# Two roots of the first batch's norms on GpSimd as a power, in an attention and MLP kernel on one core

## The chip, the core and the metric

The kernel runs on one core of a Trainium2 chip. The metric is the device time of one execution in microseconds (us). A profile is one execution recorded by the hardware profiler; its span is a little shorter than the device time of the same execution. The engines are called PE (TensorE, matrix products), ACT (ScalarE, activation functions), DVE (VectorE), POOL (GpSimd) and SP (SyncE, which here only issues DMAs). Each engine works through its own instructions in the order in which they were written and waits on semaphores for the others.

## The reference

For each of 8 batches and 12 heads, q and k (448 rows of 64) are divided by the root of their mean square and multiplied by a gain; then softmax attention over 448 keys; the heads are put side by side and pass through an MLP of 768 to 2048 to 768 with a tanh GELU.

```python
def rmsnorm(x, g):
    rms = np.sqrt(np.mean(x * x, axis=-1, keepdims=True) + 1e-06)
    return x / rms * g
q_n, k_n = (rmsnorm(q, g_q), rmsnorm(k, g_k))
scores = (1.0 / np.sqrt(64)) * np.matmul(q_n, k_n.transpose(0, 1, 3, 2))
attn = softmax(scores)                     # max subtracted, 1e-9 in the sum
x = np.matmul(attn, v)                     # to (8 * 448, 768)
h = x @ w_in
g = 0.5 * h * (1.0 + np.tanh(c * (h + 0.044715 * h * h * h)))
return g @ w_out
```

## The kernel before

The 12 heads of a batch are taken as 6 pairs, and the pairs as three chunks of two: pair `i` belongs to chunk `c = i // 2`, with `j = i % 2`. For every pair the kernel squares the raw q and k, sums the squares along the 64 elements of a row, takes the inverse root, multiplies the raw rows by it and writes bf16, transposes the result with PE, and copies it from PSUM into `qT` and `kT` (k takes the gain on the way). Then come the scores (PE, 7 tiles of 128x896 for two pairs), their exponentials (ACT), the sums over keys and the products with v (PE), reciprocals (DVE), and the product into `xT`. The MLP of a batch is interleaved with the attention of the next.

The first batch has nothing before it that could be interleaved. Its instructions are written in an order by hand, a string `FRONT` of steps that `front` (line 669) turns into instructions; each step is issued to its engine when it is read, so the string fixes the order on each engine. The steps that matter here, each followed by the number of its pair:

- `sq`, `sk`: squares of q and k (line 186 on ACT, line 188 on POOL); `tq`, `tk`: their sums on DVE (line 203).
- `rs`: the inverse root of one pair's norms, `rsqrt` (line 205): on ACT `Ln(ssq / 64 + 1e-6)` into `lg` (line 209), then `Exp(-0.5 * lg)` into `rinv` (line 212). For an even pair it covers 14 columns, for an odd one 16, of 128 partitions: 8 for q and 6 or 8 for k.
- `nk`, `nq`: the multiplication by `rinv`, written to `nrmk` and `nrmq` (line 226), on DVE (`:D`) or POOL (`:P`).
- `tpk`, `tpq`: PE transposes (lines 245 and 238); `ck`, `cq`: the copies out of PSUM on DVE (lines 264 and 255).
- `s`, `e`: scores of a tile on PE (lines 324 and 310) and their exponential on ACT (line 331); `sa`, `sb`, `xa`, `xb`: halves of the key sums and of the products with v on PE (line 370).
- `st`, `rc`, `rb`, `xt`: reciprocals and the product into `xT` on DVE (lines 377, 381, 385, 395).
- `v`, `w`, `o`, `V`: DMAs that POOL issues: v of batch 0, a quarter of `w_in` (line 630), a part of `w_out` (line 636), v of batch 1.
- `ma`, `mb`, `mc`, `md`: matrix products of the MLP of batch 0 (line 412).

The string around pairs 4 and 5, which are chunk 2:

```python
        sq4:P sq5:P w1 rc0 cq3:D rb0 ck3:D tq4 tk5 rs4 e9 xb0 s10 st1 xt0 rc1 rb1 tq5 e10 sa2
        s11 e11 rs5 nk4:P nq4:P w2 nk5:P nq5:P xa1 xb1 sb2 s12 e12 s13 tpk4 tpq4 xt1 st2 ck4:D
        cq4:D rc2 xa2 e13 rb2 sa3 xb2 s14 tpk5 tpq5 s15 e14 xt2 ck5:D cq5:D sb3 e15 U s16 s17
        xa3 xb3 s18 w3 o0 Sk0:P e16 st3 rc3 rb3 e17 xt3 e18 s19 sa4 xa4 sb4 xb4 Tk0 st4 rc4 s20
        mb0 mb1 mb2 mb3 sa5 e19 e20 o1 Sq0:P Sq1:P V0 rb4 GELU xt4 Tq0 xa5 sb5 xb5 st5 V1 V2 o2
```

`Sk`, `Sq`, `Tk`, `Tq`, `Rs` are the same squares, sums and roots for batch 1. POOL's instructions around the change are thus, in order: `sq4 sq5 w1 nk4 nq4 w2 nk5 nq5 w3 o0 Sk0 o1 Sq0 Sq1 V0 ...`, and PE's are `s12 s13 tpk4 tpq4 xa2 sa3 xb2 s14 tpk5 tpq5 s15 sb3 s16 s17 ...`. `rsqrt` is called for chunk 2 of batch 0 by `rs4` and `rs5` alone. Other batches take all their roots in one or two calls.

Of the kernel before, what the change touches and what calls it, by code (L numbers as in the profile page):

```python
# [8 lines left out]
F32 = mybir.dt.float32  # L9
BF16 = mybir.dt.bfloat16  # L10
AF = mybir.ActivationFunctionType
ALU = mybir.AluOpType
# [4 lines left out]
def kernel(  # L17
# [11 lines left out]
    nc = tc.nc  # L29
    B, H, S, D = q.shape  # L30
# [19 lines left out]
    consts = ctx.enter_context(tc.tile_pool(name="consts", bufs=1))  # L50
# [11 lines left out]
    op = ctx.enter_context(tc.tile_pool(name="op", bufs=3))  # L62
# [37 lines left out]
    kT = consts.tile([128, NCH, NS, 128], BF16)  # L100

    NU = 4 * CH + 2 * NS
    ssq = [consts.tile([128, NCH, NU], F32, name=f"ss{i}") for i in range(3)]
    raws, sqs, rinvs, nrms = {}, {}, {}, {}
    qT, xT = {}, {}
# [98 lines left out]

    def rsqrt(b, c=slice(0, NCH), at=slice(0, NU)):
        if b not in rinvs:
            rinvs[b] = smp.tile([128, NCH, NU], F32, tag="rinv", name="rinv")
        lg = smp.tile([128, NCH, NU], F32, tag="lg", name="lg")
        nc.scalar.activation(
            lg[:, c, at], ssq[b % 3][:, c, at], AF.Ln, scale=1.0 / D, bias=eps  # L210
        )
        nc.scalar.activation(rinvs[b][:, c, at], lg[:, c, at], AF.Exp, scale=-0.5)  # L212
# [397 lines left out]
    nc.vector.memset(ones, 1.0)  # L610
    nc.vector.memset(rows, 1.0)
    nc.vector.memset(ssq[0], 1.0)
    nc.gpsimd.memset(onesr, 0.0)
    for j in range(2):
        nc.gpsimd.memset(onesr[own(j), j], 1.0)
# [53 lines left out]
    def front(step):  # L669
# [7 lines left out]
        elif name in ("tq", "tk"):  # L677
            total(0, c, n, j)
        elif name == "rS":
            rsqrt(0, i, slice(0, 30))  # L680
        elif name == "rs":
            rsqrt(0, c, slice(14 * j, 14 + 16 * j))
        elif name in ("nq", "nk"):
            normed(0, c, n, j, eng)
# [46 lines left out]
        elif name == "o":  # L731
            w_out_part(i // 2, slice(i % 2 * nf // 2, (i % 2 + 1) * nf // 2))
        elif name == "L":
            loads(*divmod(i, 10))
        elif name in ("Sq", "Sk"):
            square(1, i, n, eng)
        elif name in ("Tq", "Tk"):
            total(1, i, n)
        elif name == "Rs":
            rsqrt(1, slice(0, 2))  # L740
        elif name in ("Nq", "Nk"):
            normed(1, i // 10, n, i % 10, eng)
        elif name == "Tp":
            tps["Q", i] = trans(1, i, "q", ps_o, "o")
            tps["K", i] = trans(1, i, "k", ps_m, "mm")
        elif name in ("Cq", "Ck"):
            (place_q if n == "q" else place_k)(1, i, tps[n.upper(), i], eng)
        elif name in ("GELU", "EXP"):
            nc.scalar.preload_act_table_set(EXP_SET if name == "EXP" else GELU_SET)
        elif name == "mb":  # L750
            mm1(0, [0, 1], [i], act=False)
        elif name in ("ma", "mc", "md"):
            fs = [2 * i, 2 * i + 1] if i < 7 else [i + 7]
            cs = {"ma": range(4), "mc": [4], "md": [5] if i < 3 else range(HP)}[name]
            mm1(0, fs, cs, act=False)
        elif name == "g":
            gelu(0, [2 * i, 2 * i + 1] if i < 7 else [i + 7])
        else:
            raise ValueError(step)
# [176 lines left out]
```

## Time and profile before

| what | value |
|---|---|
| time, median of 3 runs | 413.02 us (412.62 to 413.85) |
| the profiled execution's time | 413.83 us |
| its span | 412.1 us |
| mean granted clock of PE in it | 0.992 |
| busy: DVE | 274.3 us (67%) |
| busy: ACT | 296.2 us (72%) |
| busy: POOL | 131.8 us (32%) |

In the lines of the profile shown below, L226 is line 226 of the kernel. A row of a timeline gives the start in us, the duration in us, the engine, the line, the operation, what it writes and reads, how many instructions were merged into the row, and in brackets how long the engine had been idle before it and who released it. POOLq, SPq and ACTq are an engine's issuing of DMAs. A row of the chain of waits gives start, duration and what the chain ran through. The granted clock (PEclk) is the share of PE's full clock that its throttle let through. Matmuls are pipelined, so a row's duration can reach past the start of the next.

### The profile page before, as it was taken

To read this page: it belongs to the slowest core of one execution; us is meant where nothing else is said; L and a number is where in the kernel's file an instruction comes from. 1 tells how busy PE (TensorE), PEld (TensorE's weight loads), DVE (VectorE), ACT (ScalarE), POOL (GpSimd) and SP (SyncE) were. 2 spreads that over 40 slices of the span, in tenths; PEclk is the share of its full clock that TensorE was granted. 3 is DMA by queue.
4 is the path that set the end of the run, shared out by engine and by line. 5 is a ranking of instruction groups with operands and counts; after the bars stand their busy time and mean duration, and the time that the engine had idled before them with its cause. 6 is when DMAs were issued, how large, how long until landed. Compare 5 with 4: busy or idle time off the path is not lost.

```text
span 412.1 us, 10085 instructions
## 1 busy us (share of the span) xinstructions
PE 403.7 (98%) x4207; PEld 243.5 (59%) x4207; DVE 274.3 (67%) x454; ACT 296.2 (72%) x398; POOL 131.8 (32%) x144
## 2 busy tenths in 40 slices
PE   8799999999999999999999999999999999999996
PEld 3344555566655666557655666556655575556664
DVE  4899739899899638884678747786488633783010
ACT  5797987969988587767977778785976558774300
POOL 7689000234500942037500745019310460000000
PEclk9699999999999999999999999999999999999999
DMA  8999995999981689229981399616991161210022
GB/s 191 227 235 228 203 196 141 227 227 192 213 145 38 139 176 207 66 52 176 222 140 41 78 203 171 136 40 145 171 145 40 23 112 40 72 46 2 2 77 78
DMA packets 97870, 54.21 MB, mean 132 GB/s; under 512 B 63776, under 2 KB 94368, under 8 KB 97824
## 3 DMA queue, kind: packets, MB, share of 16 engines
q1 hardware_dynamic: 71392, 41.69, 43.4%
q0 software_dynamic: 26112, 11.80, 22.5%
q8 instruction: 33, 0.54, 0.6%
q10 hardware_dynamic: 320, 0.07, 0.1%
q14 instruction: 13, 0.11, 0.1%
HBM read 45.61 MB, written 11.01 MB: 137 GB/s over the span
## 4 chain that ended last, share of the span: by engine, by line
PE 95%; SPq 2%; DMA 1%; DVE 0%; ACT 0%; issue 0%; ACTq 0%; DVEq 0%
PE o L441 36%; PE hh L412 31%; PE o L370 11%; PE sc L324 8%; PE h L412 5%; PE sc L310 1%; DMA rawq<-in_q_dram 1%; PE ox L370 1%; SPq L143 1%; SPq L118 1%; SPq L136 1%; PE tp L245 0%; PE o L477 0%; PE tp L238 0%; ACT ex L331 0%
## 5 line engine op out<-in xcount | busy, mean ns | idle before, releaser
L441 PE MATMUL o<-wout,g 128*64 128x384 bf16 (+1 forms) x1648 | 160.6, 327 | 0.0
L331 ACT ACTIVATE ex<-sc,shift 128x896 bf16<-128x896 f32 x144 | 136.1, 1011 | 1.3 <-PE sc L324 1.3
L412 PE MATMUL hh<-xT,win 128*64 128x448 bf16 (+1 forms) x1260 | 133.8, 353 | 0.0
L441 PEld LDWEIGHTS <-g 128*64 128x64 bf16 (+1 forms) x1648 | 96.2, 109 | 58.3 <-issue 14.8
L412 PEld LDWEIGHTS <-win 128*64 128x64 bf16 (+1 forms) x1440 | 95.4, 109 | 49.9 <-issue 3.2
L421 ACT ACTIVATE g<-hh 128x896 bf16<-128x896 f32 x56 | 50.1, 919 | 44.5 <-PE hh L412 44.4
L203 DVE TENSOR_REDUCE ss<-sq 128x14 f32<-128x896 f32 (+4 forms) x45 | 47.9, 1080 | 32.4 <-ACT sq L186 19.9
L454 ACT COPY osb<-o 128x384 f32<-128x384 f32 x50 | 24.2, 483 | 47.8 <-PE o L441 47.8
L788 POOL COPY mark<-es 1x1 bf16<-1x1 bf16 x8 | 1.8, 225 | 162.9 <-DVE es L345 158.5
L377 DVE STREAM_TRANSPOSE st<-o 128x448 f32<-128x448 f32 x48 | 31.1, 648 | 23.6 <-PE o L370 23.2
L324 PE MATMUL sc<-qT,kT 64*128 64x448 bf16 (+1 forms) x372 | 39.6, 360 | 1.7 <-DVE kT L264 1.3
L345 DVE TENSOR_TENSOR es<-ex 128x896 bf16<-128x896 bf16 x42 | 26.8, 637 | 12.0 <-ACT ex L331 12.0
L226 POOL TENSOR_TENSOR nrmq<-rawq,rinv 112x512 bf16<-112x512 f32 x33 | 34.0, 1043 | 0.0
L226 POOL TENSOR_TENSOR nrmk<-rawk,rinv 128x512 bf16<-128x512 f32 (+1 forms) x33 | 31.1, 957 | 4.2 <-ACT rinv L212 4.2
L385 DVE STREAM_TRANSPOSE rb<-rc 128x448 f32<-128x448 f32 x48 | 31.0, 645 | 1.6
L370 PE MATMUL o<-ex,vb 128*64 128x448 bf16 x252 | 30.9, 352 | 0.0
L279 DVE TENSOR_SCALAR kT<-kT,gcol 128x896 bf16<-128x896 bf16 x19 | 21.1, 1108 | 11.7 <-DMA kT<-nrmk 11.7
L343 DVE TENSOR_TENSOR es<-es,exr 64x896 bf16<-64x896 bf16 x42 | 25.9, 617 | 2.4 <-ACT exr L331 1.0
L345 DVE TENSOR_TENSOR es<-es,ex 128x896 bf16<-128x896 bf16 x42 | 25.5, 608 | 2.3 <-ACT ex L331 0.3
L395 DVE TENSOR_TENSOR xT<-o,rb 128x448 bf16<-128x448 f32 x42 | 25.8, 615 | 1.4 <-PE o L370 0.9
L188 POOL TENSOR_TENSOR sq<-rawq 112x1024 f32<-112x1024 f32 x9 | 17.0, 1893 | 28.4 <-DMA rawq<-in_q_dram 25.0
L324 PEld LDWEIGHTS <-kT 64*128 64x128 bf16 (+1 forms) x372 | 10.9, 99 | 24.6 <-issue 18.1
(83 smaller groups left out, 349.4 us busy)
## 6 DMA issues: line engine op xcount, KB each, us to landing
rawq<-in_q_dram SPq DMA_DIRECT2D x48, 224.0 KB, 4.4
rawk<-in_k_dram SPq DMA_DIRECT2D x48, 192.0 KB, 4.6
vb<-in_v_dram POOLq DMA_DIRECT2D x8, 576.0 KB, 10.1
win<-in_moe_w_in_dram POOLq DMA_DIRECT2D x4, 768.0 KB, 14.1
wout<-in_moe_w_out_dram POOLq DMA_DIRECT2D x4, 768.0 KB, 20.4
out_dram<-osb SPq DMA_DIRECT2D x7, 336.0 KB, 4.3
out_dram<-osb SPq DMA_DIRECT2D x8, 288.0 KB, 2.7
out_dram<-osb SPq DMA_DIRECT2D x8, 240.0 KB, 2.6
```

Of the source, the lines that this page charges most:

```text
L203: nc.vector.reduce_sum(stat(ssq[b % 3], b, c, n, j), view(n, sqs[n, b, c], j), axis=AX.X)
L226: eng.tensor_mul(dst.rearrange("p t a d -> p a t d"), view(n, raws[n, b, c], j), r.to_broadcast(list(r.shape) + [D]),)
L324: nc.tensor.matmul(sc[o, a, :S], kT[r, c, 4 * j + t, o], qT[b][r, hp], start=True, stop=True,)
L331: nc.scalar.activation(dst, sc[:, :, :S], AF.Exp, scale=scale, bias=shift)
L343: nc.vector.tensor_add(es[p], es[p], exrs[b, hp // 2][p])
L345: nc.vector.tensor_add(es, ex[:, 0] if t == 1 else es, ex[:, t])
L370: nc.tensor.matmul(o[a * D:(a + 1) * D], w(a), e[:, a], start=(i == 0), stop=(i + 1 == len(steps)),)
L377: nc.vector.transpose(oas["st"].rearrange("p a b -> p (a b)"), oas[0])
L385: nc.vector.transpose(oas["rb", hp], oas["rc"].to_broadcast([128, S // 32, 32]))
L412: nc.tensor.matmul(h[i * m:(i + 1) * m, j, :S], win[:, c // 2 + NCH * (c % 2), f * 128 + i * m:f * 128 + (i + 1) * m], xT[b][:, c], start= ...
L421: nc.scalar.activation(g[:, fs[0]:fs[0] + len(fs), (b % 2) * S:(b % 2 + 1) * S], hs1[fs[0]][:, :, :S], AF.Gelu_apprx_tanh)
L441: nc.tensor.matmul(o[j * m:(j + 1) * m, :HD], g[:, f, i * 128 + j * m:i * 128 + (j + 1) * m], wout[:, f, half * HD:(half + 1) * HD], start ...
```

## The change

For chunk 2 of batch 0, so in steps `rs4` and `rs5`, the logarithm and the exponential on ACT are left out. POOL instead computes `ssq / 64 + 1e-6` into `rinv` and raises it, in place, to the power of -0.5, where the exponent is read from a constant tile `half` of 128x30 floats that POOL fills once at the beginning. The string `FRONT` stays as it is, so the new POOL instructions stand where `rs4` and `rs5` stand in it: POOL's order becomes `sq4 sq5 w1 rs4 rs4 rs5 rs5 nk4 nq4 w2 nk5 nq5 ...`. ACT has four instructions fewer; the orders on PE, DVE and SP are as before. The tile `lg` is still taken from its pool in these two calls, but not used.

```diff
     NU = 4 * CH + 2 * NS
+    half = consts.tile([128, NU], F32)
...
         lg = smp.tile([128, NCH, NU], F32, tag="lg", name="lg")
+        if b == 0 and c == 2:
+            r_ = rinvs[b][:, c, at]
+            nc.gpsimd.tensor_scalar(
+                r_, ssq[b % 3][:, c, at], 1.0 / D, 1e-6, op0=ALU.mult, op1=ALU.add)
+            nc.gpsimd.tensor_tensor(r_, r_, half[:, at], op=ALU.pow)
+            return
         nc.scalar.activation(
             lg[:, c, at], ssq[b % 3][:, c, at], AF.Ln, scale=1.0 / D, bias=eps
         )
...
     nc.vector.memset(ssq[0], 1.0)
+    nc.gpsimd.memset(half, -0.5)
     nc.gpsimd.memset(onesr, 0.0)
```

## The prediction

> **What bounds the kernel now.** I read the engines' shares and the chain of waits on the page first, then the chain in order of time, then what PE waited for.
>
> ```profile
> PE 403.7 (98%) x4207; PEld 243.5 (59%) x4207; DVE 274.3 (67%) x454; ACT 296.2 (72%) x398; POOL 131.8 (32%) x144
> PE 95%; SPq 2%; DMA 1%; DVE 0%; ACT 0%; issue 0%; ACTq 0%; DVEq 0%
> PE sc L324 <- DVE kT L264: 1.3, 1, 1.3
> ...
> PE tp L238 <- DVE nrmq L226: 1.0, 1, 1.0
> PE sc L310 <- DVE kT L264: 0.8, 1, 0.8
> PE sc L324 <- ACT ex L331: 0.4, 1, 0.4
> ```
>
> The kernel is PE: 98% busy and 95% of the chain. The other rows are all of PE's waits on other engines but the one for its first instruction. The timeline puts them in the first 22.2 us:
>
> ```profile
> 10.73 0.36 PE L324 MATMUL sc<-qT,kT 64*128 64x448 bf16 x2 [1.30 <-DVE kT L264]
> 13.36 0.37 PE L238 MATMUL tp<-ident,nrmq 112*128 112x112 bf16 x4 [1.05 <-DVE nrmq L226]
> 14.80 0.88 PE L310 MATMUL sc<-qT,kT 64*64 64x448 bf16 x4 [0.78 <-DVE kT L264]
> 22.14 0.36 PE L324 MATMUL sc<-qT,kT 64*128 64x448 bf16 x2 [0.41 <-ACT ex L331]
> ```
>
> After 22.14 PE waits for nobody to the end, so time lost on PE behind that point is lost in the total, and time saved on another engine there buys nothing. The change lies exactly there. The chain (start, duration):
>
> ```profile
> 26.61 0.27 PE tp L245 x3
> 26.89 0.20 PE tp L238 x4
> ...
> 28.64 0.33 PE tp L245 x4
> 28.97 0.20 PE tp L238 x4
> ```
>
> These are the transposes tpk4, tpq4, tpk5 and tpq5, in PE's one order. Their suppliers are POOL's four multiplications:
>
> ```profile
> 21.74 0.88 POOL L630 DMA_DIRECT2D win<-in_moe_w_in_dram  x1
> 23.52 0.82 POOL L226 TENSOR_TENSOR nrmk<-rawk,rinv 128x384 bf16<-128x384 f32 x1 [0.90 <-ACT rinv L212]
> 24.31 1.03 POOL L226 TENSOR_TENSOR nrmq<-rawq,rinv 112x512 bf16<-112x512 f32 x1
> 25.30 0.88 POOL L630 DMA_DIRECT2D win<-in_moe_w_in_dram  x1
> 26.66 1.04 POOL L226 TENSOR_TENSOR nrmk<-rawk,rinv 128x512 bf16<-128x512 f32 x1 [0.47 <-ACT rinv L212]
> 27.66 1.03 POOL L226 TENSOR_TENSOR nrmq<-rawq,rinv 112x512 bf16<-112x512 f32 x1
> ```
>
> nk4 ends at 24.34, 2.2 us ahead of tpk4; nq4 at 25.34, 1.5 ahead of tpq4; nk5 at 27.70, 0.9 ahead; nq5 at 28.69, only 0.28 ahead of 28.97 in the chain. So POOL is nearly on PE's path: whatever moves nq5 by more than about 0.28 us moves PE.
>
> **The change part by part.** Off ACT go two pairs of instructions:
>
> ```profile
> 22.88 0.30 ACT L209 ACTIVATE lg<-ss,eps 128x14 f32<-128x14 f32 x1
> 23.34 0.99 ACT L331 ACTIVATE ex<-sc,shift 128x896 bf16<-128x896 f32 x1
> 26.01 0.31 ACT L209 ACTIVATE lg<-ss,eps 128x16 f32<-128x16 f32 x1
> 26.47 1.90 ACT L331 ACTIVATE ex<-sc,shift 128x896 bf16<-128x896 f32 x2
> ```
>
> From start to start each pair takes 0.46 us, 0.92 in all. PE's last wait on ACT is at 22.14, before either, so I count 0. If that cover were gone, the most it could give is 0.92.
>
> Onto POOL come four instructions, all ahead of nk4. What matters first is their place, not their price. Before, nk4 could start once ACT had delivered the roots of pair 4 (23.52). Now rs5 stands ahead of it in POOL's order, and rs5 waits for tq5, the sum of pair 5, on DVE:
>
> ```profile
> 21.91 1.26 DVE L203 TENSOR_REDUCE ss<-g 112x8 f32<-112x512 f32 x2
> 25.18 0.64 DVE L203 TENSOR_REDUCE ss<-g 112x8 f32<-112x512 f32 x1
> ```
>
> tq5 ends at 25.82. With 0.08 us from a producer's end to POOL's start (ACT's root ended at 23.44, nk4 began at 23.52), rs5 starts at 25.90. Behind it in POOL's queue wait nk4, nq4, w2, nk5 and nq5, and PE waits for those.
>
> Prices on POOL:
>
> ```profile
> L788 POOL COPY mark<-nrmk x1: 176/176/176, 101.9 to 101.9; 1x1 bf16<-1x1 bf16 x1
> L188 POOL TENSOR_TENSOR sq<-rawq 112x1024 f32<-112x1024 f32 x9 | 17.0, 1893 | 28.4 <-DMA rawq<-in_q_dram 25.0
> ```
>
> The first is a one-element copy (least, median and longest in ns), the second the costliest arithmetic on POOL, 1.89 us each. The plain step `ssq / 64 + 1e-6` on 14 or 16 elements: the multiplications above give (1.04 - 0.82) / 128 = 1.72 ns for each element and 0.16 us that does not depend on the length, so 0.16 + 14 x 0.0017 = 0.19 us. The power, X, has no row. Its lower end is that of a plain step, 0.19; its upper end is the longest arithmetic that POOL shows, 1.89. I take X = 1.0, near the middle: a power is a logarithm and an exponential, and if these are some 35 passes over the 14 elements (the count is my guess), 35 x 14 x 1.72 ns = 0.84, with the 0.16 it is 1.0.
>
> The sum on POOL. rs4: POOL is free at 22.62, its sum tq4 ended at 21.91 + 0.63 = 22.54, so the plain step runs to 22.8 and the power to 23.8; nothing but the wait for tq5 follows, so this pair costs nothing while X is under about 25.90 - 22.8 = 3.1. rs5: 25.90 + 0.19, the power from about 26.1 to 26.1 + X. nk4 to nq5 then take what they took, 28.69 - 23.52 = 5.17, without the 0.47 of waiting for ACT in it: 4.70. nq5 ends at 30.8 + X = 31.8 instead of 28.69, 3.1 later. Less 0.28, plus 0.08 until PE starts: PE loses 2.9 us, in pieces (nk4 ends at 26.1 + 1 + 0.82 = 27.9 where tpk4 stood at 26.61, so 1.4 of it comes there; the rest before tpq4 and tpq5). With X from 0.19 to 1.89 the loss goes from 2.1 to 3.8.
>
> What follows on POOL shifts by the same 3.1: the DMAs w2, w3, o0, o1, V0 to o3, and Sk0, Sq0 and Sq1. Tightest is Sk0, whose sum Tk0 stands on DVE ahead of the reciprocals of pair 4:
>
> ```profile
> 30.42 1.70 POOL L188 TENSOR_TENSOR sq<-rawk 128x896 f32<-128x896 f32 x1
> 32.25 1.08 DVE L203 TENSOR_REDUCE ss<-sq 128x14 f32<-128x896 f32 x1
> ```
>
> Sk0 ends at 32.12, 0.13 before Tk0 starts. DVE's steps ahead of Tk0 follow PE, so they come 2.9 later and Sk0 3.1 later: the 0.13 covers all but 0.1, which I count as 0. The weights' DMAs keep their distance to PE within the same 0.2. The fill of `half` stands at POOL's start, where POOL then idles:
>
> ```profile
> 4.37 0.83 POOL L188 TENSOR_TENSOR g<-rawk 128x384 f32<-128x384 f32 x1 [0.97 <-DMA rawk<-in_k_dram]
> ```
>
> Those 0.97 us hide it; uncovered it would cost a plain step, 0.2.
>
> The second term is the clock. These stretches (length, then PE, PEld, DVE, ACT and POOL busy with their counts, granted clock, DMA share, GB/s) show what PE's gaps did once already:
>
> ```profile
> 9.00:14.00 5.00, 2.52 (x25) 1.19 (x22) 5.00 (x9) 3.46 (x7) 4.23 (x6) 1.00 1.26 225
> 14.00:20.60 6.60, 5.82 (x37) 2.35 (x36) 5.42 (x12) 5.49 (x9) 3.80 (x4) 0.50 1.37 230
> 27.00:37.00 10.00, 10.00 (x90) 4.75 (x88) 9.26 (x18) 9.67 (x11) 9.97 (x9) 1.00 1.19 230
> ```
>
> Gaps of 1.30, 1.05 and 0.78 us between 9.4 and 14.8, 3.1 us in 5.4, brought the granted clock to 0.50 for 6.6 us. The change makes gaps of the same kind: 2.9 us in pieces of 1.4 and less, between 26.9 and about 31.9. So I expect a second stretch at 0.50. Its price, from the chain at half and at full clock:
>
> ```profile
> 15.69 0.89 PE o L370 x4
> 16.58 0.48 PE sc L324 x2
> ...
> 22.51 0.50 PE o L370 x4
> ...
> 24.58 0.29 PE sc L324 x2
> ```
>
> 0.89 / 0.50 and 0.48 / 0.29 are 1.7 times as long in the mean, so a busy us at half clock does 1 / 1.7 = 0.59 us of work. Of the 6.6 us PE was busy 5.8: 5.8 x 0.41 = 2.4 lost. The lower end is 0 (the gap of 0.41 us at 22.14 brought no drop), the upper 6.6 x 0.41 = 2.7.
>
> The Trainium skill, "TensorE: Matmul & The Clock Gate", Part 1, What's actually happening, says that the clock halves after at least one idle window of about 3.4 us. By that rule gaps of 1.4 us would not halve it, and the sum would be the 2.9 alone; this trace has the 0.50 after gaps no longer than 1.30, so here the row decides.
>
> Sum: 2.9 + 2.4 = 5.3 us on the profiled span of 412.1, so 417.4, or 419.1 with the 1.7 us that lie around the span (413.83 - 412.1). That run is 0.8 above the median shown, 413.02; against the median it is 418.3.
>
> **The rivals.**
>
> 1. The same stall, no halved clock: PE loses 2.9 alone, 415.9 (2.1 to 3.8: 415.1 to 416.8). For it: the smaller gap did nothing, and ahead of the new gaps PE has been busy for 4 us where before 9.4 to 14.8 it had not been. Against: the gaps add up as they did there.
>
> 2. A power far dearer than any POOL row. From X = 3.1 on the wait for tq5 covers the first power no longer and both count: nq5 ends at 22.8 + X + 0.2 + X + 4.7 = 27.7 + 2X, and PE loses 2X - 1.2. At X = 5 that is 8.8, with the clock 11.2: 424.2. For it: no row of POOL has more than a multiplication or a copy in it, so 1.89 bounds the power only by analogy. Against: 14 elements are 1 / 73 of that row's 1024. A first use that must load something belongs here too; POOL's first multiplication (4.37, 0.83 us) is no longer than the later one of its shape (0.82), so plain operations pay nothing of the kind, and up to 2.1 us of it on the first power would be covered. The Trainium skill, "GPSIMD Engine Reference", 2.1 Instruction dispatch, gives about 6 us for the first call into a freshly loaded library; by that, an estimate, the first power would take 7, PE would lose 6.9 and with the clock the time would be 422.3. No trace here shows it.
>
> 3. Not slower: ACT, not PE, paces 27 to 37. ACT is busy 9.67 of 10 us there, and matmul ends are modelled, so PE's full row may hold hidden waits for exponentials. Then the 0.92 off ACT is gained and time is 412.1, provided that nq5's shift, 3.1, fits into slack that the rows do not show; it decides where that slack exceeds the shift. Against: no wait of PE on ACT is listed after 22.14, and the transposes wait for POOL whatever ACT does.
>
> That the change does not do what it says can be left out: the changed program has the four instructions on POOL, and ACT four fewer.
>
> **How the numbers follow.** The forecast, stall and halved clock, 0.48; rival 1, 0.30; rival 2, 0.15; rival 3, 0.05; anything else, 0.02, which I put to faster. The range goes from 415.0 (rival 1 at its lowest) to 424.0 (the beginning of rival 2 with the clock); left out are rival 3 and the upper half of rival 2, about 0.15. A measurement of this kernel tells about 0.3%, 1.2 us, from no change: rival 3 (0.9 less) falls within it, the forecast and rivals 1 and 2 are slower: faster 0.02, same 0.05, slower 0.93.
>
> **What would show it.** The waits: POOL's plain step of rs5 waits for DVE's L203, and PE's transposes wait for POOL's nrmk and nrmq, 2.9 us in all, where none were listed. POOL: the two powers' lengths give X; nq5 ends near 31.8. The granted clock: a second stretch near 0.50 between about 30 and 38, and a mean under 0.992. ACT: exponentials back to back at 22.9 and 26.0. The forecast is wrong if nq5 ends before about 29, if PE shows gaps but the end does not move with them, or if a power exceeds 3 us.

## The result and the profile after

| what | before | changed |
|---|---|---|
| time, median of 4 runs | 412.82 us (412.42 to 413.85) | 419.18 us (418.2 to 419.52) |
| the profiled execution, its span | 413.83, 412.1 us | 419.5, 417.7 us |
| mean granted clock in it | 0.992 | 0.986 |

The changed kernel is slower: ratio 1.0146, 95% interval 1.012 to 1.0173. The mean clock by itself says little: in one set of the kernel before, five of 13 runs have 0.986 or 0.987 too, and take no longer (412.97 to 413.4). On the page of the changed kernel (its lines are numbered up to eight higher: 233 stands for 226, 252 for 245, 245 for 238, 204 for 203, 331 for 324, 338 for 331) the shares of the engines and of the chain:

```profile
PE 405.4 (97%) x4207; PEld 243.8 (58%) x4207; DVE 273.5 (65%) x454; ACT 295.5 (71%) x394; POOL 138.4 (33%) x149
PE 92%; DMA 5%; SPq 2%; issue 0%; POOL 0%; DVE 0%; ACTq 0%; ACT 0%; DVEq 0%; POOLq 0%
```

POOL has 6.6 us more to do and ACT four instructions less. The 5% that the chain now gives to DMAs are loads of k between 8.3 and 29.2 us: the chain is led back to them from nq4, although it is POOL's own order that holds nq4, and no wait of PE or POOL on a load is listed just ahead of it. The new waits of PE on other engines, from the list of waits (us, times, longest), and the rows of POOL that they go back to:

```profile
PE tp L252 <- POOL nrmk L233: 3.4, 1, 3.4
...
PE tp L245 <- POOL nrmq L233: 0.7, 1, 0.7
```

```profile
22.62 0.21 POOL L212 TENSOR_SCALAR rinv<-ss 128x14 f32<-128x14 f32 x1
22.92 2.63 POOL L214 TENSOR_TENSOR rinv<-rinv,half 128x14 f32<-128x14 f32 x1
25.83 0.21 POOL L212 TENSOR_SCALAR rinv<-ss 128x16 f32<-128x16 f32 x1 [0.28 <-DVE ss L204]
26.12 2.92 POOL L214 TENSOR_TENSOR rinv<-rinv,half 128x16 f32<-128x16 f32 x1
28.99 0.83 POOL L233 TENSOR_TENSOR nrmk<-rawk,rinv 128x384 bf16<-128x384 f32 x1
29.78 1.04 POOL L233 TENSOR_TENSOR nrmq<-rawq,rinv 112x512 bf16<-112x512 f32 x1
...
32.71 1.05 POOL L233 TENSOR_TENSOR nrmq<-rawq,rinv 112x512 bf16<-112x512 f32 x1
```

The plain steps cost 0.21 us, the powers 2.63 and 2.92. The second root waits for DVE's sum of pair 5, but only 0.28 us, since the first power fills nearly all of that time. nk4 starts at 28.99 instead of 23.52, and nq5 ends at 33.76 instead of 28.69: 5.07 us late. PE in the same stretch:

```profile
25.97 0.55 PE L331 MATMUL sc<-qT,kT 64*128 64x448 bf16 x4
29.88 0.34 PE L252 MATMUL tp<-ident,nrmk 128*128 128x128 bf16 x3 [3.36 <-POOL nrmk L233]
30.88 0.52 PE L245 MATMUL tp<-ident,nrmq 112*128 112x112 bf16 x4 [0.66 <-POOL nrmq L233]
...
34.21 0.45 PE L252 MATMUL tp<-ident,nrmk 128*128 128x128 bf16 x4
34.50 0.36 PE L245 MATMUL tp<-ident,nrmq 112*128 112x112 bf16 x4
```

tpk4 waits 3.36 us and tpq4 0.66, 4.0 together. Then no wait is listed for tpk5 and tpq5, though nk5 and nq5 are late as well: PE itself is slow now. The stretches (length, busy us of PE, PEld, DVE, ACT and POOL with counts, granted clock, DMA share, GB/s):

```profile
20.60:31.00 10.40, 5.97 (x53) 2.40 (x54) 6.59 (x13) 6.72 (x8) 9.88 (x10) 0.99 1.19 237
31.00:34.20 3.20, 3.20 (x18) 1.17 (x16) 1.55 (x4) 0.00 (x0) 3.17 (x4) 0.50 1.14 256
34.20:44.00 9.80, 9.80 (x82) 4.67 (x81) 8.78 (x16) 8.63 (x9) 9.77 (x9) 0.99 1.24 209
```

The clock was at 0.50 for some 3.4 us: in windows of 0.4 us it falls at about 30.95 and is back at about 34.4. tpq5 starts 0.74 us after nq5's end (33.76 to 34.50), where before it started 0.11 after (28.69 to 28.80). So tpq5 is 5.70 us late, 5.07 of it POOL's and 0.63 the slow clock's, and the span is 5.6 longer: nothing comes back later.

ACT's part can be seen too. Before, it ran without a break from 28.68 to 35.07; now it idles for PE:

```profile
26.38 1.90 ACT L338 ACTIVATE ex<-sc,shift 128x896 bf16<-128x896 f32 x2 [0.43 <-PE sc L331]
34.37 2.80 ACT L338 ACTIVATE ex<-sc,shift 128x896 bf16<-128x896 f32 x3 [6.09 <-PE sc L331]
```

### The profile page after: what moved, and what is told of

It reads as the page before. It is cut to its first block, busy times and chain, and to the rows that moved or that the text cites. A ratio compares the mean times of both kernels' runs of the same rounds, so it can differ in the third digit from the quotient of the medians.

```text
span 417.7 us, 10086 instructions
## 1 busy us (share of the span) xinstructions
PE 405.4 (97%) x4207; PEld 243.8 (58%) x4207; DVE 273.5 (65%) x454; ACT 295.5 (71%) x394; POOL 138.4 (33%) x149
## 4 chain that ended last, share of the span: by engine, by line
PE 92%; DMA 5%; SPq 2%; issue 0%; POOL 0%; DVE 0%; ACTq 0%; ACT 0%; DVEq 0%; POOLq 0%
PE o L448 35%; PE hh L419 31%; PE o L377 10%; PE sc L331 8%; DMA rawk<-in_k_dram 5%; PE h L419 5%; PE sc L317 1%; PE ox L377 1%; SPq L144 1%; SPq L119 1%; SPq L137 0%; PE o L484 0%; PE tp L245 0%; POOL nrmq L233 0%; PE tp L252 0%
## 5 line engine op out<-in xcount | busy, mean ns | idle before, releaser
L286 DVE TENSOR_SCALAR kT<-kT,gcol 128x896 bf16<-128x896 bf16 x19 | 19.9, 1049 | 13.0 <-DMA kT<-nrmk 12.8
```

## The experiments

A step `y` with a number, in some of the strings below, is that many products of zeros on PE.

The theory at this point: PE sets the end, nq5 is nearly on its path, so time is lost by (1) the second root's place ahead of nk4, (2) the price of the power, (3) the clock that PE's gaps bring down; ACT's relief brings nothing. The rivals: only one of these counts; or ACT sets the pace in 27 to 37.

The first 24 us of an execution vary: s12, which with s13 is the last score product ahead of tpk4, starts at 24.10 in one kernel and at 26.06 in another, and at 24.15 and 25.77 in two executions of the same one (e5_fill and e5b_fill). Where parts of a us matter I therefore read from s12's start to tpq5's start, which holds all four waits for POOL: 2.74 us in the kernel before (26.06 to 28.80), 8.53 in the changed one.

| kernel | s12 to tpq5 | lost against 2.74 | tpq5 to the end | ratio to before, 95% interval |
|---|---|---|---|---|
| before | 2.74 | | 383.3 | |
| changed | 8.53 | 5.79 | 383.2 | 1.0146 (1.012 to 1.0173) |
| a2_after, the changed kernel again | 8.23 | 5.49 | 383.6 | 1.0149 (1.0131 to 1.0166) |
| e1_cheap | 5.12 | 2.38 | 383.6 | 1.0067 (1.0051 to 1.0084) |
| e1b_cheap, the same again | 5.12 | 2.38 | 383.7 | 1.0074 (1.006 to 1.0088) |
| e8_cheapfill | 5.12 | 2.38 | 383.2 | 1.0061 (1.0048 to 1.0074) |
| e2_order | 7.34 | 4.60 | 386.4 | 1.0174 (1.0155 to 1.0193) |
| e3_pair4 | 4.75 | 2.01 | 383.6 | 1.005 (1.0035 to 1.0065) |
| e4_noroot | 2.74 | 0.00 | 383.2 | 1.0002 (0.9992 to 1.0011) |
| e5_fill | 8.41 | 5.67 | 383.7 | 1.0112 (1.0097 to 1.0127) |
| e5b_fill | 7.84 | 5.10 | 384.1 | 1.0135 (1.0119 to 1.0151) |
| e6_warm | 2.74 | 0.00 | 383.9 | 1.0003 (0.9991 to 1.0015) |

The column "tpq5 to the end" scatters from 383.2 to 384.1 without a cause that I found; 386.4 is outside of that. The column "s12 to tpq5" has an uncertainty of its own: POOL's first step for pair 4 starts 3.35 us ahead of s12 in the changed kernel, but 2.59 in e5_fill, 3.08 in e3_pair4 and 3.82 in e2_order. Where POOL then waits for the sum of pair 5 (changed, a2_after, e1_cheap, e1b_cheap, e5b_fill, e8_cheapfill), this makes no difference; in the three named it does, and their losses are good to some half a us only.

**e1_cheap: the place without the price.**

```diff
-                r_, ssq[b % 3][:, c, at], 1.0 / D, 1e-6, op0=ALU.mult, op1=ALU.add)
-            nc.gpsimd.tensor_tensor(r_, r_, half[:, at], op=ALU.pow)
+                r_, ssq[b % 3][:, c, at], -0.5 / D, 1.5, op0=ALU.mult, op1=ALU.add)
+            nc.gpsimd.tensor_tensor(r_, r_, half[:, at], op=ALU.mult)
...
-    nc.gpsimd.memset(half, -0.5)
+    nc.gpsimd.memset(half, 1.0)
```

> The changed kernel with the power replaced by a multiplication of the same shape on GpSimd (the roots become a straight-line approximation), so the place of the two steps stays and their price goes from 2.6 and 2.9 us to about 0.2. If place matters by itself: the second step still waits for the sum of pair 5, nq5 ends near 31.0 instead of 28.7, PE loses about 2.1 us, span near 414.2, and 415.8 to 416.6 if the clock halves again. If only the price of the power matters: no loss, span within 0.5 of 412.1.

POOL's timeline in this kernel:

```profile
21.40 0.22 POOL L214 TENSOR_TENSOR rinv<-rinv,half 128x14 f32<-128x14 f32 x1
23.95 0.21 POOL L212 TENSOR_SCALAR rinv<-ss 128x16 f32<-128x16 f32 x1 [2.33 <-DVE ss L204]
24.24 0.22 POOL L214 TENSOR_TENSOR rinv<-rinv,half 128x16 f32<-128x16 f32 x1
24.42 0.83 POOL L233 TENSOR_TENSOR nrmk<-rawk,rinv 128x384 bf16<-128x384 f32 x1
```

All of POOL's four new instructions are at most 0.23 us, and yet POOL stands idle for 2.33 us until DVE has summed pair 5, with nk4 behind it. PE loses 2.38 us (2.1 was expected), most of it in three listed gaps of 0.66, 0.66 and 0.60. The place alone costs; that only the price matters is refuted. No stretch at 0.50 followed these short gaps in the profiled execution.

**e2_order: the price without the place.**

```diff
-        s11 e11 rs5 nk4:P nq4:P w2 nk5:P nq5:P xa1 xb1 sb2 s12 e12 s13 tpk4 tpq4 xt1 st2 ck4:D
+        s11 e11 nk4:P nq4:P w2 rs5 nk5:P nq5:P xa1 xb1 sb2 s12 e12 s13 tpk4 tpq4 xt1 st2 ck4:D
```

> The changed kernel with the second root moved behind nk4, nq4 and the DMA w2, so that nk4 does not wait for the sum of pair 5. If the price sets the time: GpSimd has as much to do as before the move and never idles, nq5 ends near 33.4, PE loses about 4.5 us without the clock, span 416.6 to 418.5. If the wait for the sum of pair 5 is the main cause: at least 2 us come back, span at most 415.5.

It did not come back: 1.0174, no faster than the changed kernel, with whose interval its own overlaps. nk4 and nq4 are early enough now, but the powers are still on POOL and nq5 behind them; PE stands at tpk5 instead:

```profile
31.21 0.40 PE L252 MATMUL tp<-ident,nrmk 128*128 128x128 bf16 x4 [3.35 <-POOL nrmk L233]
32.21 0.56 PE L245 MATMUL tp<-ident,nrmq 112*128 112x112 bf16 x4 [0.60 <-POOL nrmq L233]
```

The loss to tpq5 is 4.60, so the price alone is enough for nearly all of it, and place and price do not add up (2.38 and 4.60 against 5.07 for nq5): the wait for tq5 lies beside the first power. The stretches show what came on top:

```profile
24.20:31.50 7.30, 3.71 (x37) 1.65 (x33) 3.76 (x8) 3.56 (x4) 7.06 (x7) 1.00 1.18 238
31.50:38.30 6.80, 6.20 (x34) 1.89 (x34) 3.89 (x7) 3.84 (x5) 6.77 (x6) 0.53 1.19 234
```

The halved clock begins at about 31.9, after the long gap, lasts for some 6.8 us and lies almost wholly behind the last wait for POOL, so it counts in full: from tpq5 to the end 386.4 instead of 383.3, 3.1 us (2.3 to 3.2 against the other rows of the table).

**e3_pair4: one power only.** The condition becomes `if b == 0 and c == 2 and at.start == 0`, so pair 5 keeps its roots on ACT.

> The changed kernel with the power for pair 4 alone; pair 5 is left to ScalarE. The first power ends near 25.6, nk4 to nq5 follow without a gap, nq5 ends near 30.3: PE loses 1.4 us in two gaps of under 1 us, span near 413.5 without a halved clock. If a halved clock follows even such small gaps: 415 or more. If the first power is free, as the prediction had it: span 412.1.

The loss is 2.01, ratio 1.005: the first power is not free. There is no second root to wait for, so the time that hid it in the prediction is not there either; nk4 begins at 24.10, right after the power of 2.63 us, and nq5 ends at 28.87. I had expected 1.4; POOL reached the root 0.36 us later against s12 than in the profile of before, and the 0.28 us of slack that the 1.4 takes off was not there, as shown further below. In the changed kernel itself the first power was covered, as predicted: POOL still idled 0.28 us for the second root.

**e4_noroot: ACT's relief alone.**

```diff
             rinvs[b] = smp.tile([128, NCH, NU], F32, tag="rinv", name="rinv")
+            if b == 0:
+                nc.vector.memset(rinvs[b][:, 2], 1.0)
+        if b == 0 and c == 2:
+            return
```

> The kernel before, with the roots of pairs 4 and 5 left out (their factors are set to one), so ScalarE loses the same four instructions and GpSimd gets nothing. If PE sets the pace there, as the prediction has it: span within 0.3 us of 412.1. If ScalarE does (rival 3): 0.9 us less.

Ratio 1.0002 (0.9992 to 1.0011), and 2.74 us from s12 to tpq5, as before. ACT does not set the pace there: rival 3 is refuted, and ACT's relief can win nothing that these runs show.

**e5_fill and e5b_fill: PE kept busy in the gap.** The same edit in two sets of runs, the second beside the changed kernel on one chip.

```diff
-        ... s12 e12 s13 tpk4 tpq4 xt1 st2 ck4:D
+        ... s12 e12 s13 y30 tpk4 y6 tpq4 xt1 st2 ck4:D
```

> The changed kernel with 30 products of zeros ahead of tpk4 and 6 ahead of tpq4, so that PE is busy in the gap that waits for GpSimd. If PE's idle time halves the clock: no stretch at 0.50 after 24 us, PE reaches tpk5 early and waits for nq5 (end near 33.8), so the loss falls from 5.7 to about 4.9 us from s12 to the end, time near 417.8. If the halved clock has another cause or costs nothing: stretch at 0.50 as before and 419 or more.

> e5_fill once more, beside the changed kernel on the same chip. If PE's idle time halves the clock and that costs time: 0.3 to 1.4 us less than the changed kernel, no stretch at 0.50 after 24 us. If the halved clock is covered by the wait for nq5: the same time within 0.3.

> The changed kernel once more, beside e5b_fill on one chip: near 1.0146 of the kernel before.

Medians: e5_fill 417.92; e5b_fill 418.11 beside 419.06 for a2_after, the changed kernel again (1.0149, 1.0131 to 1.0166). The last two intervals overlap, so the times alone do not settle it; the traces do. In e5b_fill:

```profile
26.25 3.05 PE L224 MATMUL w<-zeros 128*128 128x224 bf16 x30
29.68 0.34 PE L252 MATMUL tp<-ident,nrmk 128*128 128x128 bf16 x3 [0.38 <-POOL nrmk L233]
...
33.61 0.37 PE L245 MATMUL tp<-ident,nrmq 112*128 112x112 bf16 x4 [0.60 <-POOL nrmq L233]
```

```profile
32.51 1.04 POOL L233 TENSOR_TENSOR nrmq<-rawq,rinv 112x512 bf16<-112x512 f32 x1
```

```profile
24.00:44.00 20.00, 18.93 (x164) 10.25 (x161) 14.28 (x28) 12.45 (x13) 19.64 (x18) 1.00 1.21 231
```

With products of zeros in the gap the clock stays at 1.00 to 44, and tpq5 starts 0.06 us after nq5's end (33.55) instead of 0.74; in e5_fill it is 0.05, with no stretch at 0.50 after 24 us either. a2_after has the slow stretch again, from about 30.7 to 34.1:

```profile
31.95 1.04 POOL L233 TENSOR_TENSOR nrmq<-rawq,rinv 112x512 bf16<-112x512 f32 x1
33.44 0.58 PE L245 MATMUL tp<-ident,nrmq 112*128 112x112 bf16 x4
```

There tpq5 starts 0.45 us after nq5's end. So PE's idle time does bring the clock down, and that costs the changed kernel 0.68 us in one profile and 0.39 in the other; the rest of the slow stretch is covered by the wait for nq5.

**e6_warm: the slow stretch that was there already.**

```diff
-        ... tq2 s0 e0 y3 s1 ... e1 tpk1 tpq1 s2 ... ck1:D cq1:D s3 e3 ...
+        ... tq2 y11 s0 e0 y3 s1 ... e1 tpk1 y9 tpq1 s2 ... ck1:D cq1:D y6 s3 e3 ...
```

> The kernel before, with 11, 9 and 6 products of zeros in the three gaps of PE between 9.4 and 14.8 us (ahead of s0, tpq1 and s3). If those gaps cause the stretch at 0.50 and PE sets the pace from 15 us on: no such stretch, up to 2.4 us less, time near 410.5. If the loads of q and k set the pace of these first 22 us: the clock stays full and the time stays within 0.5 of 412.9.

```profile
14.00:20.60 6.60, 5.54 (x47) 2.37 (x46) 6.57 (x15) 6.30 (x11) 3.80 (x5) 1.00 1.35 226
```

The stretch at 0.50 that began at 14.0 is gone, and the time is what it was (413.0 beside 413.11; the interval leaves room for a gain of 0.4 us at most). In the profiled execution s12 starts at 24.58 instead of 26.06, but e4_noroot has it at 24.53 with the clock at 0.50 for as long as before, so the times of all runs decide. The chain in order of time suggests why; between 8 and 20 us it runs through DVE and ACT, and these are among its longest pieces:

```profile
11.10 0.60 DVE nrmk L226
11.70 1.45 DVE nrmq L226
...
14.79 0.90 ACT ex L331
15.68 0.90 ACT exr L331
...
17.03 2.70 ACT ex L331 x3
```

Both of what I had set against each other missed it: neither the loads nor PE at its full clock pace this part.

**e7_price: the power by itself.** In the kernel before, seven powers on a scratch tile after 40 us, where POOL has nothing to do; in order `128x14, 128x14, 128x16, 128x1, 128x8, 128x20, 16x14`.

> The kernel before, with seven powers on a scratch tile while GpSimd has nothing else to do (after 41 us): 128x14 twice, 128x16, 128x1, 128x8, 128x20, 16x14. If the price goes with the columns: some 0.146 us for each over about 0.6, so 2.6, 2.6, 2.9, 0.7, 1.8 and 3.5, and the sixteen partitions cost as much as the 128. If the first power pays for loading its code: the first 128x14 is longer than the second. If it goes with all elements: 16x14 at an eighth of 2.0 plus 0.6. Time as the kernel before.

From POOL's timeline, one row for each, and one row of the tile's list for 128x1, the least of its two (least, median, longest in ns):

```profile
40.12 2.62 POOL L782 TENSOR_TENSOR pw<-pw 128x14 f32<-128x14 f32 x1
42.83 2.83 POOL L782 TENSOR_TENSOR pw<-pw 128x14 f32<-128x14 f32 x1
45.73 2.90 POOL L782 TENSOR_TENSOR pw<-pw 128x16 f32<-128x16 f32 x1
49.34 2.12 POOL L782 TENSOR_TENSOR pw<-pw 128x8 f32<-128x8 f32 x1
51.53 3.53 POOL L782 TENSOR_TENSOR pw<-pw 128x20 f32<-128x20 f32 x1
55.14 2.57 POOL L782 TENSOR_TENSOR pw<-pw 16x14 f32<-16x14 f32 x1
...
L782 POOL TENSOR_TENSOR pw<-pw x2: 547/1723/2899, 45.7 to 48.7; 128x16 f32<-128x16 f32 x1, 128x1 f32<-128x1 f32 x1
```

From 1 to 20 columns the price goes from 0.55 to 3.53 us, 0.157 us a column on average, though not on a straight line (8 columns cost 2.12, where the line gives 1.65). Sixteen partitions cost as much as 128. The first power of this kernel is no longer than the second, so no row shows a first use that pays for a load.

**e1b_cheap and e8_cheapfill: short gaps filled.** e1_cheap again, and with `y6` ahead of tpk4 and of tpq4.

> e1_cheap once more, beside e8_cheapfill: near 1.0067 of the kernel before, with the mean granted clock changing from run to run between 0.992 and 0.987.

> e1_cheap with 6 products of zeros ahead of tpk4 and 6 ahead of tpq4, in gaps of 0.66 us each. If such short gaps halve the clock in some runs: the loss falls from 2.7 us towards 2.0 and no run has a stretch at 0.50 after 24 us. If they never do: the same time as e1b_cheap within 0.3.

Ratios 1.0074 (1.006 to 1.0088) and 1.0061 (1.0048 to 1.0074); both profiles have 5.12 us from s12 to tpq5 and no stretch at 0.50 after 24 us. The medians, 416.13 and 415.3, differ by more than I allowed for "the same", the intervals overlap, and the mean clock varies by run in both (0.987 to 0.992, 0.988 to 0.992), as it does in the kernel before. The clock does not explain the difference: three runs of e1b_cheap with 0.992 take 415.87 to 416.13, hardly less than the 416.27 of the one with 0.987. Whether these gaps of 0.66 us ever halve the clock stays open.

## Why the prediction was right, and where its terms were not

The forecast was 418.3 against 419.18 measured, a stall and a halved clock. Of its mechanism the stall held point by point, and the halved clock came, though not behind the gaps that it was expected from; the two terms were mis-sized, in opposite directions.

- PE sets the end and passes everything on: tpq5 is 5.70 us late against the profile of before, and the span 5.6 longer.
- ACT's four instructions are worth 0: shown by e4_noroot.
- The second root's place ahead of nk4 costs by itself: forecast 2.1 with a cheap power, 2.38 in e1_cheap.
- The power, X, was taken as 1.0 with an upper end of 1.89; it is 2.63 and 2.92. This is the term that failed. The upper end was POOL's longest multiplication, and nothing made a power of 14 columns comparable with it: the multiplications gave 1.72 ns for each element, and the power takes some 157 for each column (e7_price). The sum on POOL was sound: nq5's end at 30.8 + X is 33.7 with X = 2.92, and 33.76 was measured. With X known, the same working gives a stall of 4.8 instead of 2.9. The boundary of rival 2, X = 3.1, was nearly reached: POOL idled 0.28 us between the roots, 0.40 in a2_after, and not at all in e5_fill.
- The slack of 0.28 us that the sum takes off was not there. It was read from the chain, which has tpq5 at 28.97; in the timeline it starts at 28.80, 0.11 after nq5's end, and e5b_fill shows that PE needs some 0.06 of that. So the stall is about 5.1, the loss of e5b_fill, and not 4.8; the same 0.28 separates the 2.38 of e1_cheap from the 2.1 forecast.
- The halved clock came where it was expected (from 31.0, forecast between about 30 and 38), but for 3.4 us and not 6.6, and most of it was covered by the wait for nq5. It cost 0.4 to 0.7 instead of 2.4. The step that failed is the price: I multiplied the slow stretch's busy time by its slowness, without asking whether PE would have had to wait anyway. e6_warm shows that the stretch from which I took the price cost nothing that its runs can tell, and its chain, through DVE and ACT, suggests why; e2_order shows the full price of a stretch of 6.8 us, some 3 us, where nothing covers it.
- That the clock fell at all was forecast from pieces of 1.4 us and less that add up. The piece that came ahead of it was 3.36 us long, because X was so large; that the smaller pieces would have done it is not shown, and the profiles with three gaps of 0.60 to 0.66 have no drop after them. So the drop was met partly by luck. The working from the first drop needs a correction too: of its three gaps the last (14.02 to 14.80) begins when the clock has just fallen, at 14.0, so only 1.30 and 1.05 lie ahead.
- So 2.9 + 2.4 = 5.3 stood for 5.07 + 0.63 = 5.7. The total came close because the errors cancelled, not because the terms were right.
- The upper end of the range, 424.0, is not what it is called: the beginning of rival 2 with the clock, X = 3.1, gives 413.02 + 5.0 + 2.4 = 420.4, and 424.0 stands for X near 4.9.

On the clock, the rule cited from the Trainium skill, "TensorE: Matmul & The Clock Gate", Part 1, would have been met here by the 3.36 us gap, which is about the idle window that it names; the gaps of 0.66 in e1_cheap and e1b_cheap brought no stretch at 0.50 in either profile, as the rule would have it, while the stretch at 14.0 us before, after gaps of 1.30 and less, does not fit it as I read it. Nor does the stretch that begins at 11.4 us in e1_cheap itself, where the listed gaps ahead of it are 0.79 and 0.90 us; in the 3.4 us ahead of these two drops PE was busy for 2.1 and 1.8 us. But between 24.6 and 28.0 in e1_cheap it was busy for 2.1 us too, with no drop, so no bound follows from these figures.

## What to carry to other kernels

An instruction put on an in-order engine costs first by what it waits for and who stands behind it: cheap steps of 0.2 us cost 2.4 us here, because the second of them waited for a sum that the instruction behind it did not need. Taking work off an engine that the bottleneck does not wait for brings nothing, and a function that no row shows should get an upper end well above the engine's plain instructions. A slow-clock stretch is priced only over the time in which the matrix engine would not have waited anyway.

## What the runs showed of the hardware

- A GpSimd power costs about 0.16 us for each column, on 16 partitions as on 128: 2.62 us for 128x14, where ACT's logarithm and exponential of that shape took 0.46 from start to start, and a GpSimd multiplication 0.22.
- The granted clock fell to 0.50 in stretches of about 3.4 us (30.95 to 34.4 in the changed kernel, 30.7 to 34.1 in a2_after, 15.3 to 18.7 in e3_pair4) or 6.8 us (14.0 to 20.8 before, 31.9 to 38.8 in e2_order), read from windows of 0.4 us. So it seems to be set in steps of some 3.4 us; that a stretch ends only on such a step was not tested.
- Products of zeros in PE's idle time keep the clock at 1.00; in e6_warm its mean over the execution is 1.0 (0.992 before).
